# Products 6, 3 and 1 first for every expert, and one more wait for GpSimd's sums of w2

## The chip, the cores and the metric

The kernel runs on one core of one Trainium2 chip. The metric is the time of one execution on the device in microseconds (us), median of several runs. The core has TensorE (PE; its weight loads are PEld in the profile), VectorE (DVE), ScalarE (ACT), GpSimd (POOL), and SyncE (SP), which issues most DMAs.

## What is computed

Block-sparse attention (4 batches, 8 heads, 768 positions, 64 wide), and on its output x (3072 x 512) a mixture of 8 experts in which every token goes through every expert, weighted by a balanced gate P:

```python
logits = x @ w_gate
P = np.exp(logits - logits.max())
for _ in range(8):
    P /= P.sum(1, keepdims=True) + 1e-09
    P /= P.sum(0, keepdims=True) + 1e-09
    P *= N / E
for e in range(E):
    h = np.maximum(x @ w1[e], 0.0)
    out += P[:, e:e + 1] * (h @ w2[e])
```

w1 is 8 x 512 x 1024, w2 is 8 x 1024 x 512, all in fp32.

## The kernel before

**Attention** takes the first 412 us or so. Its order is written out by hand, and the change does not touch it: up to the last attention matmul all five engines have the same instructions in the same order before and after.

**The experts** follow as 32 tiles: tile i is expert e = i // 4 and batch b = i % 4 (768 tokens). Both layers use Strassen's scheme in Winograd's form: the operands are cut into 2 x 2 quadrants, and 7 products of sums of quadrants (named 0 to 6) take the place of 8. Every fp32 operand is split into a high and a low fp16 half, and a product takes three matmuls for each pair of blocks (high x high, high x low, low x high).

*First layer* (`stage1(i)`): each of the 7 products has 4 pieces q = 0 to 3 of 128 rows of h; one is a group of 6 matmuls of 384 columns into one of five PSUM banks `p_0` to `p_4` (line L1710; the pool "s1"). After a product a bank is read by ScalarE (`scaled_copy`, L1692, which starts a "pair" tile) or by VectorE (`scaled_add`, L1683, which adds the bank to a pair tile), and the next product adds to what stands in the same bank, so it waits for that reading. For experts 2 to 7 the products 6, 3, 1 and 2 are cut a second time into 7 inner products each (`inner_product`, STEPS, groups of 6 matmuls of 192 columns, L1739); they read further sums of w1 and x, kept in `loft`. `twos(e)` says which products that is: none for experts 0 and 1, (6, 3, 1, 2) for the others.

The other products run in an outer part: g = 0 takes q = 0, 1 and g = 1 takes q = 2, 3. Before, experts 0 and 1 take 0, 1, 5, 6, 4, 3, 2 there, for g = 0 and then for g = 1, without any overlap of the tiles' first layers. Experts 2 to 7 take 6, 3, 1, 2 as inner products first, and then 0, 5, 4; the half g = 1 is kept back and merged into product 6 of the next tile. `tokens()` writes this order down.

From the sums in the pair tiles (r, u, c; the bank itself holds a until all that needs it is done) ScalarE, VectorE and GpSimd make h with its own sums, as high halves (L1939, ScalarE) and low halves (L1930 on VectorE or L1928 on GpSimd, one or the other by the planner's choice). There are nine pair tiles and 24 h tiles.

*Second layer* (`stage2(i)`): 7 products in the order 1, 0, 5, 6, 3, 4, 2, each for 3 blocks of 128 tokens, a group of 12 matmuls of 256 columns (L2062) into one of three banks `y_0` to `y_2`. Results go to `acc` tiles and to DRAM.

**Weights.** `fetch_w1(e)` and `fetch_w2(e)` load a matrix into the one buffer `raw_w`, find its largest magnitude (8 pieces on ScalarE, L363; the maxima over the partitions go to DRAM and back as `peak_d` and `peaks`), make the sums of quadrants on GpSimd (`tts`, L1453) and split each product into `w1p[p]` or `w2p[p]` (high: ScalarE, L1465; low: VectorE, L1470). Product p of expert e can be split only when the last matmul of expert e - 1 on product p has run. For the inner products `inner(p, ...)` adds four sums on GpSimd and a second split (L1511, L1516). In `fetch_w2` the sums `d5` for product 5 write over m00, product 0's source, and wait for `zero`, product 0's split; `one` is product 1's split.

**x tiles.** `load_x(i + 1)` reloads the seven `xp[p]` from DRAM (L487), each after its last matmul in tile i. `prep_x` makes the inner sums of x once for the 16 pairs of batch and product (L1636 to L1673).

**The order on the engines** is set by a planner (`Plan.run`). It simulates the engines with fixed costs per job, takes on each engine the job with the earliest due time among those that are ready, and the instructions are then written in the order that comes out. On the chip each engine goes through its list in that order. SLK is the time after a group's planned end at which its bank shall have been read, SLK2 the same for the second layer, SHIFT the distance of the second layer behind the first, EASE an allowance for each group, MARGIN a factor on all costs but PE's and the DMAs', PREP0, PREP1 and PREPD the due times of `prep_x`.

Of the kernel before, what the change touches and what calls it, by code (L numbers as in the profile page):

```python
# [35 lines left out]
SLK, SLK2, SHIFT, EASE, SOON = 4, 2, 10, 0.2, 120.0  # L36
SLK3 = 20.0
PREP0, PREP1, PREPD = 100, 210, 50
# [3 lines left out]
LOADED = 5.0  # L42
WARM0, WARM1, WARM2 = 19, 5, 22
# [24 lines left out]
class Plan:  # L68
# [3 lines left out]
    MARGIN = 1.05  # L72
# [237 lines left out]
def tile_sparse_attention_moe(  # L310
# [1230 lines left out]
    def fetch_w2(e, loaded=None, done=None):  # L1541
# [26 lines left out]
        d5 = tts(m00, m11, t1, h2, tuple(zero), 0.73)  # L1568
# [127 lines left out]
    def stage1(i):  # L1696
# [140 lines left out]
        one, many, last = 1 in two, 6 in two, 2 in two  # L1837
        got = {}
        if many:
            got[6] = inner_product(6)  # L1840
            got[3] = inner_product(3, got[6])
        if one:
            got[1] = inner_product(1)
        if last:
            got[2] = inner_product(2)

        for g in range(NF // 2):
# [28 lines left out]
            first = lambda t, q: (t,)  # L1876
            prior = {}
            for q, (j, end) in outer(0, X, True, {}).items():
                if one:
                    r_[q] = scaled_add(cell(R, q), bank(X[q]), cell(R, q), [j] + rdep, dl=end + SLK)  # L1880
                    prior[q] = (r_[q],)
                else:
                    k = scaled_copy(cell(R, q), bank(X[q]), (j,), take=first(R, q), dl=end + SLK)
                    prior[q] = (k,)
            if not one:
                Z = {q: hold("s1") for q in qis}
                for q, (j, end) in outer(1, Z, True, {}).items():
                    r_[q] = scaled_add(
                        cell(R, q), bank(Z[q]), cell(R, q), (j,) + prior[q], drop=(Z[q],), dl=end + SLK
                    )  # L1890
            if not many:
                Y = {q: hold("s1") for q in qis}
            k5, k6 = {}, {}
            for q, (j, end) in outer(5, X, False, prior).items():
                if many:
                    c_[q] = scaled_add(cell(C, q), bank(X[q]), cell(C, q), [j] + cdep, dl=end + SLK)
                    k5[q] = c_[q]
                else:
                    k5[q] = scaled_copy(cell(C, q), bank(X[q]), (j,), take=first(C, q), dl=end + SLK)
# [369 lines left out]
```

## Time and profile before

| what | us |
|---|---|
| time, median of 3 runs (2136.47 to 2137.1) | 2136.53 |
| the profiled execution, its own time | 2137.5 |
| the span of that profile | 2135.7 |
| PE busy | 2113.9 |
| DVE busy | 1727.2 |
| ACT busy | 1431.2 |
| POOL busy | 1123.5 |

The span is what lies between the first and the last instruction; the 1.8 us between it and the execution's own time is not in the rows. Times in the rows are us from the span's start. A busy PE is a matmul in its pipeline: the end that a row shows for a group is about 0.16 us later than the moment at which the next group could begin, so an idle time of PE in a row is that much shorter than the gap between two groups.

### The profile page before, as it was taken

Reading aid. Unit: us, or ns where it says so; the run is one execution under the profiler, and the core shown is the slowest. Engines: PE = TensorE matmul, PEld = TensorE weight load, DVE = VectorE, ACT = ScalarE, POOL = GpSimd, SP = SyncE. Lnnn points to the kernel's source line nnn. Section 1 sums busy time; section 2 is a strip of 40 time slices with the busy share of each in tenths; the row PEclk is TensorE's granted clock in tenths of the full one; section 3 lists DMA queues with packets and bytes.
Section 4 is the critical chain, followed back from the end, with each engine's and each line's share of the span. In section 5 each row is a group of like instructions: output and inputs, shape, how many; then the busy total and the mean of one; then the engine's idle time right before and its main releaser. Section 6 shows DMA issues by size and latency. Waiting matters only on the chain.

```text
span 2135.7 us, 51438 instructions
## 1 busy us (share of the span) xinstructions
PE 2113.9 (99%) x20619; PEld 1711.2 (80%) x20619; DVE 1727.2 (81%) x3141; ACT 1431.2 (67%) x2785; POOL 1123.5 (53%) x1308
## 2 busy tenths in 40 slices
PE   9999999999999999999999999999999999999999
PEld 6777676667777778888888888888888888888888
DVE  8878889799778868877887888788878887888776
ACT  6788888886677656766676667656765676676442
POOL 6456768555345527644554456445644564456333
PEclk9999999999999999999999999999999999999999
DMA  7767866444446644464556455645554555455432
GB/s 160 146 137 160 213 137 141 149 125 139 150 154 188 183 135 146 152 148 112 136 129 153 112 139 126 151 112 146 124 146 112 151 129 136 112 166 150 142 97 68
DMA packets 225092, 299.79 MB, mean 140 GB/s; under 512 B 134332, under 2 KB 154708, under 8 KB 224852
## 3 DMA queue, kind: packets, MB, share of 16 engines
q1 hardware_dynamic: 218528, 265.02, 44.4%
q0 software_dynamic: 5760, 31.46, 9.1%
q8 instruction: 161, 2.64, 0.5%
q14 instruction: 79, 0.65, 0.1%
q10 hardware_dynamic: 564, 0.03, 0.0%
HBM read 198.15 MB, written 67.64 MB: 124 GB/s over the span
## 4 chain that ended last, share of the span: by engine, by line
PE 92%; DVE 4%; ACT 2%; DMA 1%; POOL 1%; issue 1%; SPq 0%; DVEq 0%; ACTq 0%
PE y L2062 41%; PE p L1710 23%; PE p L1739 15%; PE u L1056 4%; PE t L994 2%; PE t L989 2%; PE m L956 2%; PE m L959 2%; DVE top L965 1%; DMA qt<-qs 1%; ACT pe L999 0%; ACT unread L363 0%; PE u L1090 0%; POOL loft L548 0%; DVE pl L1009 0%
## 5 line engine op out<-in xcount | busy, mean ns | idle before, releaser
L2062 PE MATMUL y<-w2p,h 128*128 128x256 f16 x8064 | 980.7, 273 | 0.9 <-DVE h L1930 0.8
L2062 PEld LDWEIGHTS <-h 128*128 128x128 f16 x8064 | 784.5, 98 | 120.1 <-DVE h L1930 1.1
L1928 POOL TENSOR_TENSOR h<-pair,h 128x384 f16<-128x384 f32 x383 | 386.9, 1024 | 495.2 <-ACT h L1939 447.6
L1924 ACT ACTIVATE pair<-pair 128x384 f32<-128x384 f32 x384 | 198.2, 519 | 241.4 <-DVE pair L1683 239.9
L1710 PE MATMUL p<-arena 128*128 128x384 f16 x1728 | 322.3, 326 | 1.9 <-DVE pair L1683 1.9
L1939 ACT ACTIVATE h<-pair 128x384 f16<-128x384 f32 x640 | 303.7, 514 | 25.2 <-POOL pair L1970 13.2
L2101 DVE SCALAR_TENSOR_TENSOR acc<-y,spare,acc 128x256 f32<-128x256 f32 x408 | 201.6, 496 | 124.9 <-PE y L2062 116.6
L1683 DVE SCALAR_TENSOR_TENSOR pair<-p,pair 128x384 f32<-128x384 f32 x384 | 212.1, 553 | 81.3 <-PE p L1710 74.3
L1710 PEld LDWEIGHTS <-arena 128*128 128x128 f16 x1728 | 167.1, 98 | 84.6 <-issue 2.4
L999 ACT ACTIVATE pe<-t,qk 128x768 int32<-128x768 f32 x192 | 172.3, 899 | 64.5 <-PE t L994 57.2
L1710 PE MATMUL p<-attic 128*128 128x384 f16 x1152 | 213.6, 326 | 0.0
L1739 PEld LDWEIGHTS <-loft 128*128 128x128 f16 x2304 | 199.1, 98 | 16.2 <-issue 1.3
L965 DVE TENSOR_REDUCE top<-m 128x1 f32<-128x768 f32 x192 | 181.5, 951 | 37.4 <-PE m L959 36.4
L1930 DVE SCALAR_TENSOR_TENSOR h<-pair,h 128x384 f16<-128x384 f32 x257 | 187.0, 748 | 18.7 <-ACT h L1939 17.2
L1710 PEld LDWEIGHTS <-attic 128*128 128x128 f16 x1344 | 130.7, 98 | 66.4
L1739 PE MATMUL p<-loft 128*128 128x192 f16 x1728 | 181.3, 246 | 0.0
L1692 ACT ACTIVATE u<-p 128x384 f32<-128x384 f32 x216 | 105.5, 488 | 99.5 <-PE p L1739 75.8
L2089 ACT ACTIVATE acc<-y,spare 128x256 f32<-128x256 f32 (+1 forms) x180 | 97.7, 543 | 88.9 <-PE y L2062 79.4
L1453 POOL TENSOR_TENSOR raw_w<-raw_w 128x256 f32<-128x256 f32 (+1 forms) x150 | 130.4, 881 | 32.9 <-DVE attic L1470 14.7
L1013 POOL TENSOR_SCALAR pl<-pe 128x768 f16<-128x768 uint16 x109 | 93.3, 859 | 78.0 <-ACT pe L999 75.9
L989 PE MATMUL t<-qt,kt 128*128 128x512 f16 (+1 forms) x384 | 124.9, 325 | 3.6 <-DVE top L965 2.9
L1928 POOL TENSOR_TENSOR h<-u,h 128x384 f16<-128x384 f32 x91 | 89.9, 998 | 72.5 <-ACT h L1939 55.4
(249 smaller groups left out, 3856.4 us busy)
## 6 DMA issues: line engine op xcount, KB each, us to landing
arena<-xd SPq DMA_DIRECT2D x128, 384.0 KB, 3.8
attic<-xd SPq DMA_DIRECT2D x96, 384.0 KB, 3.3
loft<-xsd SPq DMA_DIRECT2D x96, 384.0 KB, 4.9
accd<-acc POOLq DMA_DIRECT2D x40, 768.0 KB, 9.1
raw_w<-in_moe_w_dram SPq DMA_DIRECT2D x28, 1024.0 KB, 5.7
accd<-acc SPq DMA_DIRECT2D x16, 768.0 KB, 4.1
acc<-accd SPq DMA_DIRECT2D x16, 768.0 KB, 4.4
xd<-loft SPq DMA_DIRECT2D x28, 384.0 KB, 2.9
```

What stands on the lines that cost most here:

```text
L965: nc.vector.tensor_reduce(out=tops[n][:, c : c + 1], in_=sc[:, :S], axis=AX.X, op=ALU.max)
L989: nc.tensor.matmul(sc[:, lo:hi], lhsT=kt[:, 0, c], rhs=qa[:, lo:hi], start=True, stop=False)
L999: nc.scalar.activation(pe, sc[:, :S], AF.Exp, bias=EXP_SHIFT, scale=qk[n // 2][3])
L1683: lambda: nc.vector.scalar_tensor_tensor(out=out_(), in0=bank_(), scalar=HDOWN, in1=add(), op0=ALU.mult, op1=ALU.add),
L1710: nc.tensor.matmul(bk.tile[:, :TH], lhsT=w1p[p][:, l, kc, fs], rhs=xp[p][:, r, kc], start=(fresh and kc == 0 and m == 0), stop=(kc == KH - ...
L1739: nc.tensor.matmul(bk.tile[:, c * HT : (c + 1) * HT], lhsT=lhs(l, c), rhs=rhs(rr), start=(fresh and c == 0 and m == 0), stop=(m == 2), ski ...
L1924: return job({"ACT": 0.52}, lambda: nc.scalar.activation(view(), view(), AF.Relu), dep)
L1928: nc.gpsimd.tensor_tensor(out=out_, in0=x, in1=y, op=ALU.subtract)
L1930: nc.vector.scalar_tensor_tensor(out=out_, in0=x, scalar=1.0, in1=y, op0=ALU.mult, op1=ALU.subtract)
L1939: lambda: nc.scalar.activation(h.tile[:, 0], src(), AF.Relu if relu else AF.Copy),
L2062: nc.tensor.matmul(py, lhsT=hh[i, p, kc].tile[:, l, tsl], rhs=w2p[p][:, r, kc], start=(old is None and kc == 0 and m == 0), stop=(kc == h2 ...
L2101: lambda dst=dst, src=src, t=t: nc.vector.scalar_tensor_tensor(out=dst(), in0=src(), scalar=pwe[e][:, t : t + 1] if e else 1.0, in1=dst(), ...
```

## The change

- For experts 0 and 1 the new function `front` runs product 6 and, in the same bank, product 3, first for q = 0, 1 and then for q = 2, 3; then it runs product 1 alone. ScalarE evacuates each of these pieces into pair tiles (6 pair tiles of a tile, as for experts 2 to 7). The outer part is now 0, 5, 4, 2 for these experts, with VectorE adding the bank to the pair tile after 0, 5 and 4 and ScalarE taking the bank after 2. A tile has as many matmuls, copies and adds as before.
- `tokens()` keeps back the half g = 1 for all experts and merges it into the products 6 and 3 of the next tile, from expert 1 to expert 2 too.
- `load_x` asks for 6, 3, 1, 2, 0, 5, 4 in this order.
- `d5` waits for `one` too.
- Constants: SLK 4 to 2.5, SLK2 2 to 5, SHIFT 10 to 11, EASE 0.2 to 0.3, PREP0 100 to 80, PREP1 210 to 170, MARGIN 1.05 to 1.08. DIRECT = 4 is new; it is compared with b, which is at most 3, so that `weighs` is `e` and `fresh` is as before.

```diff
-SLK, SLK2, SHIFT, EASE, SOON = 4, 2, 10, 0.2, 120.0
+SLK, SLK2, SHIFT, EASE, SOON = 2.5, 5, 11, 0.3, 120.0
...
-PREP0, PREP1, PREPD = 100, 210, 50
+PREP0, PREP1, PREPD = 80, 170, 50
...
+DIRECT = 4
...
-    MARGIN = 1.05
+    MARGIN = 1.08
...
-        d5 = tts(m00, m11, t1, h2, tuple(zero), 0.73)
+        d5 = tts(m00, m11, t1, h2, tuple(zero) + tuple(one), 0.73)
...
-        for p in PORDER:
+        for p in (6, 3, 1, 2, 0, 5, 4):
...
+        def front(chain):
+            sets = [[hold("pair") for _ in range(2)] for _ in chain]
+            made_ = [{}, {}]
+            for g in range(NF // 2):
+                qis = (2 * g, 2 * g + 1)
+                Y = {q: hold("s1") for q in qis}
+                prior = {q: () for q in qis}
+                for n, p in enumerate(chain):
+                    for q in qis:
+                        deps = list(prior[q])
...
+                        j, end = pe(
+                            (p, "q", q), start_group(p, q, Y[q], n == 0), NOUT, deps,
+                            take=(Y[q],) if n == 0 else (),
+                        )
...
+                        k = scaled_copy(
+                            lambda t=t, q=q: t.tile[:, q % 2], lambda q=q, Y=Y: Y[q].tile[:, :TH], (j,),
+                            take=(t,), drop=(Y[q],) if n == len(chain) - 1 else (), dl=end + SLK,
+                        )
+                        prior[q] = (k,)
...
+        if 6 in two:
             got[6] = inner_product(6)
             got[3] = inner_product(3, got[6])
-        if one:
+        else:
+            front((6, 3))
+        if 1 in two:
             got[1] = inner_product(1)
+        else:
+            front((1,))
...
-                steps = [p for p in (0, 1, 5, 6, 4, 3, 2) if p not in two]
+                steps = [p for p in (0, 5, 4, 2) if p not in two]
...
-            if 6 in two and 1 in two:
-                order += merge(inner[6], kept)
-                order += merge(inner[1], inner[3])
-                order += merge(inner.get(2, []), outer[0])
-                kept = outer[1]
+            if 6 in two:
+                order += merge(quarters[6], kept)
+                order += merge(lead[1], quarters[3])
             else:
-                order += kept
-                kept = []
-                for p in (6, 3, 1, 2):
-                    order += inner.get(p, [])
-                order += outer[0] + outer[1]
+                front = [t for g in (0, 2) for p in (6, 3) for t in halves(p, (g, g + 1))]
+                order += merge(front, kept)
+                order += lead[1]
+            order += merge(lead[2] if 2 in two else [], outer[0])
+            kept = outer[1]
         return order + kept
```

Lines after the change stand one later (L1692 is L1693) up to `front`, and six or seven later behind it (L1930 is L1936, L1970 is L1976, L2062 is L2069).

**Place A: ScalarE at the start of expert 0**, from the first split of the last x tile on (L1303 and L1304, into `loft`). L1692 and L1693 evacuate a bank `p`, L363 and L364 are pieces of w2's magnitude. Before:

```order
L1303 ACTIVATE loft_83<-loft_83 128x768 x2
L1692 ACTIVATE pair_0_8096<-p_0_8064 128x384
L1303 ACTIVATE loft_83<-loft_83 128x768
L1692 ACTIVATE pair_0_8096<-p_1_8065 128x384
L363 ACTIVATE unread_76,mx_w2_0_8172<-raw_w_4332 128x512 x3
L1692 ACTIVATE pair_1_8097<-p_0_8064 128x384
L363 ACTIVATE unread_76,mx_w2_0_8172<-raw_w_4332 128x512 x2
```

After:

```order
L1304 ACTIVATE loft_83<-loft_83 128x768
L1693 ACTIVATE pair_0_8096<-p_0_8064 128x384
L1304 ACTIVATE loft_83<-loft_83 128x768
L1693 ACTIVATE pair_0_8096<-p_1_8065 128x384
...
L1693 ACTIVATE pair_1_8097<-p_0_8064 128x384
L364 ACTIVATE unread_76,mx_w2_0_8171<-raw_w_4332 128x512
```

The bank `p_0`, product 0 before and product 6 after, is read after one split in place of two, and the evacuations stand between single pieces of the magnitude.

**Place B: PE in tile 0, from g = 0 to g = 1**, the first matmul of each group. Before, the rows are 2 (q = 0, 1; banks p_0 and p_1), 0 (q = 2, 3), 1 (q = 2; q = 3 follows in the same bank p_3) and 5 (q = 2):

```order
L1710 MATMUL p_0_8064<-attic_91 128x384
...
L1710 MATMUL p_1_8065<-attic_91 128x384
...
L1710 MATMUL p_4_8068<-arena_87 128x384
...
L1710 MATMUL p_2_8066<-arena_87 128x384
...
L1710 MATMUL p_3_8067<-arena_87 128x384
```

After, they are 2 (q = 0, 1; banks p_4 and p_0), then in turn product 6 of tile 1 (p_1), 0 of tile 0 for q = 2 (p_3), 6 of tile 1 (p_2), and 0 of tile 0 for q = 3:

```order
L1711 MATMUL p_4_8068<-attic_91 128x384
...
L1711 MATMUL p_0_8064<-attic_91 128x384
...
L1711 MATMUL p_1_8065<-arena_87,attic_91 128x384
...
L1711 MATMUL p_3_8067<-arena_87 128x384
...
L1711 MATMUL p_2_8066<-arena_87,attic_91 128x384
...
L1711 MATMUL p_4_8068<-arena_87 128x384
```

The last of these rows writes again the bank in which a of q = 0 stands (first row); before, the bank that was written twice in a row was p_3, with product 1.

**Place C: PE from expert 1 to expert 2**, the first matmul of each group. L1739 and L1740 are quarter products of tile 8. Before, from the last half product of tile 7 on:

```order
L1710 MATMUL p_4_8068<-attic_91 128x384
...
L2062 MATMUL y_2_8071<-w2p_4_8061,h_2_8074 128x256
...
L1739 MATMUL p_2_8066<-arena_87,attic_91 128x192
...
L1739 MATMUL p_3_8067<-arena_87,attic_91 128x192
...
L2062 MATMUL y_0_8069<-w2p_2_8059,h_3_8075 128x256
```

After, from the first quarter product of tile 8 on (L1711 are product 0 of tile 7 for q = 3 and product 5 for q = 2):

```order
L1740 MATMUL p_4_8068<-arena_87,attic_91 128x192
...
L1711 MATMUL p_3_8067<-arena_87 128x384
...
L2069 MATMUL y_1_8070<-w2p_5_8062,h_6_8078 128x256
...
L1740 MATMUL p_0_8064<-arena_87,attic_91 128x192
...
L2069 MATMUL y_2_8071<-w2p_5_8062,h_6_8078 128x256
...
L1711 MATMUL p_1_8065<-arena_87 128x384
```

Tile 8 begins while tile 7 still has seven of its half products ahead, at product 5 of the second layer of tile 6 in place of product 2, and its quarter products stand among those of tile 7.

## Rows read from the trace of the kernel before

**Rows 1.** The page's first two lines of busy time (span; each engine's busy time, share and instruction count) and the row of the clock that TensorE was granted in 40 slices of the span, in tenths.
```profile
span 2135.7 us, 51438 instructions
PE 2113.9 (99%) x20619; PEld 1711.2 (80%) x20619; DVE 1727.2 (81%) x3141; ACT 1431.2 (67%) x2785; POOL 1123.5 (53%) x1308
...
PEclk9999999999999999999999999999999999999999
```

**Rows 2.** The page's chain of work that ended last, its shares by engine.
```profile
PE 92%; DVE 4%; ACT 2%; DMA 1%; POOL 1%; issue 1%; SPq 0%; DVEq 0%; ACTq 0%
```

**Rows 3.** Busy time in stretches of 20 us: the stretch, its length, then busy us and instruction count of PE, PEld, DVE, ACT and POOL, the granted clock, the DMA share and GB/s. The start of expert 0, a stretch of expert 0 at speed, the change from expert 1 to expert 2, and the end.
```profile
420.00:440.00 20.00, 18.78 (x116) 11.20 (x115) 14.55 (x29) 19.60 (x51) 8.62 (x10) 1.00 0.41 84
...
460.00:480.00 20.00, 20.00 (x157) 15.13 (x156) 18.92 (x34) 13.42 (x28) 10.18 (x10) 1.00 0.51 166
...
820.00:840.00 20.00, 19.17 (x180) 16.67 (x178) 17.61 (x30) 15.32 (x27) 17.94 (x17) 1.00 0.58 197
...
940.00:960.00 20.00, 19.30 (x188) 16.98 (x186) 13.54 (x30) 8.78 (x20) 5.30 (x7) 1.00 0.84 193
...
2120.00:2140.00 20.00, 12.47 (x115) 10.93 (x112) 5.26 (x11) 0.00 (x0) 0.00 (x0) 0.93 0.18 60
```

**Rows 4.** Whom PE waited for, in us, number of waits and the longest, asked for four stretches one after the other: 398 to 470 us, 820 to 850, 850 to 900, 930 to 965. From 470 to 820 us PE waited for nobody.
```profile
PE p L1710 <- DVE pair L1683: 1.9, 2, 1.2
...
PE y L2062 <- DVE h L1930: 0.8, 1, 0.8
...
PE p L1739 <- DVE pair L1814: 0.3, 1, 0.3
...
PE p L1739 <- DVE pair L1814: 0.7, 1, 0.7
```

**Rows 5.** The chain of work that ended last, in order of time (start us, us, engine and line, matmuls): two whole groups of the second layer, two half products, four quarter products, each running without a gap.
```profile
582.98 2.62 PE y L2062 x24
589.83 1.95 PE p L1710 x12
...
1102.57 1.98 PE p L1739 x24
```

**Rows 6.** PE's timeline at the start of expert 0 (start us, us with the pipelined end of the last matmul, line, operation, tile, matmuls, and in brackets the idle time before).
```profile
411.87 1.14 PE L1710 MATMUL p<-arena 128*128 128x384 f16 x6
...
413.82 4.06 PE L1710 MATMUL p<-arena 128*128 128x384 f16 x24
...
427.10 3.09 PE L1710 MATMUL p<-arena 128*128 128x384 f16 x18
431.41 3.08 PE L1710 MATMUL p<-arena 128*128 128x384 f16 x18 [1.22 <-DVE pair L1683]
...
442.13 3.09 PE L1710 MATMUL p<-arena 128*128 128x384 f16 x18
445.94 0.32 PE L1710 MATMUL p<-arena 128*128 128x384 f16 x1 [0.72 <-DVE pair L1683]
```

**Rows 7.** ScalarE's timeline at the same place: the two copies of the last attention head, the first splits of the last x tile, an evacuation, and one of the eight pieces of w2's largest magnitude.
```profile
413.70 0.87 ACT L1100 ACTIVATE loft<-y 128x384 f32<-128x384 f32 x2 [3.02 <-PE y L1090]
414.45 1.58 ACT L1303 ACTIVATE loft<-loft 128x768 f16<-128x768 f32 x2
415.92 0.49 ACT L1692 ACTIVATE pair<-p 128x384 f32<-128x384 f32 x1
...
417.39 0.65 ACT L363 ACTIVATE unread<-raw_w 128x512 bf16<-128x512 f32 x1
```

**Rows 8.** VectorE's timeline there: the low halves of two splits, a sum in a bank, one low half of h alone, two of them beside GpSimd, and the reduction that waits for w2's peaks.
```profile
415.33 1.83 DVE L1306 TENSOR_TENSOR loft<-loft 128x768 f16<-128x768 f32 x2 [2.27 <-ACT loft L1303]
...
428.27 0.56 DVE L1970 TENSOR_TENSOR p<-p,pair 128x384 f32<-128x384 f32 x1
...
432.21 0.54 DVE L1930 SCALAR_TENSOR_TENSOR h<-u,h 128x384 f16<-128x384 f32 x1
...
433.61 1.82 DVE L1930 SCALAR_TENSOR_TENSOR h<-pair,h 128x384 f16<-128x384 f32 x2
...
439.88 0.28 DVE L459 TENSOR_REDUCE ma_w<-peaks 128x1 f32<-128x128 f32 x1
```

**Rows 9.** GpSimd's timeline beside the two low halves that stand last but one in rows 8.
```profile
432.66 0.92 POOL L1928 TENSOR_TENSOR h<-pair,h 128x384 f16<-128x384 f32 x1 [0.32 <-ACT h L1939]
433.83 1.19 POOL L1970 TENSOR_TENSOR pair<-pair,pair 128x384 f32<-128x384 f32 x1 [0.26 <-DVE pair L1970]
```

**Rows 10.** SyncE's queue: w2's peaks of expert 0 go out to DRAM and come back.
```profile
424.72 0.32 SPq L1435 DMA_DIRECT2D peak_d<-ma_w  x1
...
434.50 0.32 SPq L1439 DMA_DIRECT2D peaks<-peak_d  x1
```

**Rows 11.** w1 of expert 2, in order of time: the first split on ScalarE, the split of product 6 on ScalarE, and from the chain of waits the low half of the inner sums of product 1 on VectorE.
```profile
800.36 1.14 ACT L1465 ACTIVATE arena<-raw_w,sw 128x1024 f16<-128x1024 f32 x1
...
811.45 1.14 ACT L1465 ACTIVATE attic<-s,sw 128x1024 f16<-128x1024 f32 x1
...
845.69 2.04 DVE loft L1516
```

**Rows 12.** VectorE's longest stand at an x tile in 455 to 830 us (us, times, longest), and a low half of w2 of expert 0 on its timeline.
```profile
DVE loft L1636 <- DMA loft<-xd: 1.9, 1, 1.9
...
443.27 1.28 DVE L1470 SCALAR_TENSOR_TENSOR w2p<-raw_w,sw,w2p 128x1024 f16<-128x1024 f32 x1
```

More of the change, by code (lines that the diff above doesn't have):

```diff
@@ L1852, in stage1 @@
             M, mdep = made(2) if last else (None, [])
-            R, rdep = made(1) if one else (hold("pair"), [])
-            C, cdep = made(3) if many else (hold("pair"), [])
-            U, udep = made(6) if many else (hold("pair"), [])
+            R, rdep = made(1)
+            C, cdep = made(3)
+            U, udep = made(6)
             cell = lambda t, q: (lambda: t.tile[:, q % 2])
@@ L1874, in outer @@
                 return res
-            first = lambda t, q: (t,)
             prior = {}
             for q, (j, end) in outer(0, X, True, {}).items():
[L1879 to L1890, printed above, removed]
@@ L1891, in stage1 @@
-            if not many:
-                Y = {q: hold("s1") for q in qis}
-            k5, k6 = {}, {}
-            for q, (j, end) in outer(5, X, False, prior).items():
[L1895 to L1899, printed above, removed]
-            if not many:
-                for q, (j, end) in outer(6, Y, True, {}).items():
-                    k6[q] = scaled_copy(cell(U, q), bank(Y[q]), (j,), take=first(U, q), dl=end + SLK)
@@ L1903, in stage1 @@
-            for q, (j, end) in outer(4, X, False, {q: (k5[q],) for q in qis}).items():
-                u_[q] = scaled_add(
-                    cell(U, q), bank(X[q]), cell(U, q), [j] + (udep if many else [k6[q]]), dl=end + SLK
-                )
-                ends[q] = end
-            if not many:
-                for q, (j, end) in outer(3, Y, False, {q: (k6[q],) for q in qis}).items():
-                    c_[q] = scaled_add(
-                        cell(C, q), bank(Y[q]), cell(C, q), (j, k5[q]), drop=(Y[q],), dl=end + SLK
-                    )
+                r_[q] = scaled_add(cell(R, q), bank(X[q]), cell(R, q), [j] + rdep, dl=end + SLK)
@@ L1913, in stage1 @@
+                prior[q] = (r_[q],)
+            for q, (j, end) in outer(5, X, False, prior).items():
+                c_[q] = scaled_add(cell(C, q), bank(X[q]), cell(C, q), [j] + cdep, dl=end + SLK)
+            for q, (j, end) in outer(4, X, False, {q: (c_[q],) for q in qis}).items():
+                u_[q] = scaled_add(cell(U, q), bank(X[q]), cell(U, q), [j] + udep, dl=end + SLK)
+                ends[q] = end
             if last:
@@ L2025, in stage2 @@
         loaded = {}
-        fresh = e == 0 or ADDS <= e < NE - 1
+        fresh = e == 0 or ADDS <= e < NE - 1 or e == 1 and b >= DIRECT
+        weighs = e or b >= DIRECT
         if not fresh:
@@ L2089, in stage2 @@
                         lambda dst=dst, src=src, t=t: nc.scalar.activation(
-                            dst(), src(), AF.Copy, scale=pwe[e][:, t : t + 1] if e else 1.0
+                            dst(), src(), AF.Copy, scale=pwe[e][:, t : t + 1] if weighs else 1.0
                         ),
-                        rd + ([weighed[e]] if e else []), take=take, drop=drop, dl=at + SLK2,
+                        rd + ([weighed[e]] if weighs else []), take=take, drop=drop, dl=at + SLK2,
                     )
@@ L2101, in stage2 @@
                         lambda dst=dst, src=src, t=t: nc.vector.scalar_tensor_tensor(
[L2102 removed]
+                            out=dst(), in0=src(), scalar=pwe[e][:, t : t + 1] if weighs else 1.0,
                             in1=dst(), op0=ALU.mult, op1=ALU.add,
```

19 lines of the change are left out of this document (14 added, 5 removed).

## The prediction

> **What bounds the kernel now.** I read the page's busy times first: PE is busy for 2113.9 of 2135.7 us, no other engine for more than 81%, and TensorE's clock was granted in full in all 40 slices [rows 1], the higher of its two levels. The chain of work that ended last is PE for 92% [rows 2]. So the question is not which engine is fast, but where PE stands still, and the stretches of 20 us tell it [rows 3]: 20.00 of 20 us busy at 460 us, but 18.78 at 420, 19.17 at 820, 19.30 at 940, and the end. From 470 to 820 us PE waits for nobody [rows 4]. Where it runs, a group takes what its columns cost: 2.62 us for two groups of 12 x 256 columns (1.31 each), 1.95 for two of 6 x 384 (0.975), 1.98 for four of 6 x 192 (0.495) [rows 5]. The change leaves the number of groups of each kind as it is, so this part of the time, nearly all of it, can't move. What can move is the standing time around the experts, and of that there is little. At the start, PE waits twice for VectorE's reading of a bank, 1.22 and 0.72 us as shown [rows 6]. A shown idle time is 0.16 us too short: a group of 1.14 us in its row takes 0.975. The real gaps are thus 1.38 and 0.88, together **2.26**. From expert 1 to expert 2 PE waits 0.8, 0.3 and 0.7 [rows 4]; with 3 x 0.16 about **2.3**. The sum is 4.6 us, 0.2% of the time. That is the most that an order of the experts' work can give back, and 0.2% is also about what a measurement of this kernel can tell from no change. The end of the program (12.47 us busy in its last slice [rows 3]) has the same order before and after and stays.
>
> **The new front of experts 0 and 1.** The work per tile is the same: 28 groups of 0.975 and 21 of 1.31 us, 54.8 us, in experts 0 and 1. What is new is who has to be quick. Product 3 now adds to product 6's bank, so the third group of the first tile waits for ScalarE's copy of the first. Before, the second group of the same bank came seven groups of work later or had a bank of its own. I follow the start of tile 0 by hand, with the durations of the rows and the new order.
>
> (a) Product 6 for q = 0 starts at 411.87 as the first group does now, q = 1 starts at 413.82 and ends at 414.80 [rows 6]. ScalarE ends the last head's copies at 414.45, then makes one split of the x tile (1.58 for two, 0.79) and then the copy (0.49) [rows 7]: 414.45 + 0.79 + 0.45 = about 415.7. PE wants to begin product 3 at 414.80: a gap of 0.87. The copy of q = 1 stands behind a second split: 415.7 + 0.79 + 0.45 = 416.9 against 416.6 or so at which PE is through with q = 0 of product 3: I take 0.14. Later pieces of w2's magnitude (0.65 a piece [rows 7]) stand singly between the copies, and the groups alternate between banks, so that a copy has 0.975 + 0.975 us; no gap. Sum **1.0**.
>
> (b) From g = 0 to g = 1 (Place B) product 0 for q = 3 overwrites p_4, where a of q = 0 stands until VectorE has read it for the last time. On VectorE the sums there stand in this order behind the relu of both banks: the sum in p_4, then the reading of product 0 for q = 2, the sum in p_0, the low half from p_4, the low half of an x split, and only then the last reading of p_4. The second of these waits for PE's own group, product 0 for q = 2. From that group's end VectorE needs 0.56 + 0.56 + 0.54 + 0.92 + 0.56 = 3.1 us (a sum, a sum, a low half, half of the 1.83 for two splits' low halves, a sum) [rows 8], while PE has one group between (product 6 of tile 1, 0.975). Gap 3.1 - 0.98 = **2.2**.
>
> Together 3.2 in place of 2.26: **+0.9**. That tile 0's second layer begins some 8.5 us later costs nothing, since first-layer groups of tile 1 fill the place. The reduction that waits for w2's peaks stood at 439.88, 15.2 us after the peaks went out at 424.72 [rows 8, 10]. After, they go out about 3 us later, so the answer would be there at about 443, which is about when VectorE comes to it: no stall that PE sees. Bounds for the start as a whole: -1.3 (if the low half of x has run ahead and neither gap of (b) opens) to +2.5 (if the x split meets GpSimd's work).
>
> **VectorE beside GpSimd.** Two low halves of h took 1.82 us where one alone took 0.54, while GpSimd ran a low half of 0.92 and a sum of 1.19 beside them [rows 8, 9]; 0.74 us were lost. The Trainium skill, "SBUF — State Buffer", section "🔬 SBUF: two separate sides", has a rule for it: VectorE and GpSimd share a pair of ports that one instruction holds for itself, and the loser waits for all of it. That rule speaks against this change, and the row agrees with it: the loss is not a few per cent of a bandwidth. Four of the five steps in (b) read a bank and not two SBUF tiles; the x split does read two. Were it held up by one whole sum of GpSimd (1.19), the gap would be 3.4; this is a rival below.
>
> **From expert 1 to expert 2.** Before, tile 8's quarter products begin only when tile 7's first layer is through, the second layer's work between them is short, and PE comes too soon for the h tiles and for the sums in the bank [rows 4]. w1 of expert 2 is split from 800.36 on, product 6 is split at 811.45 and the inner sums of product 1 end at 845.69 + 2.04 [rows 11]. After, product 6 is last read by expert 1 near 763 us, 3 near 771 and 1 near 781 (groups counted from the start at their durations), and the first quarter product comes near 801, with seven half products of tile 7 and its second layer to mix in (Place C). Counted in the same way in the two orders (the durations of [rows 5]), tile 7's second layer then stands 12.5 and 19.9 us behind the last groups that its first two products need, the distances of the regular tiles where PE waits for nobody [rows 4]; before they were 9.7 and 13.6. So the three waits should go: **-2.3**. I leave **+0.3** for one short wait that stays. Bounds: -2.3 to +1 (a new wait for the inner sums, of the length of one of them, 2.04 [rows 11], half hidden).
>
> **Inside experts 0 and 1.** Here nothing can be gained, only lost. Each merged piece is followed on its bank after 2.3 to 3.7 us, some 6.9 before, counted likewise (at the nearest, in tile 0, 0.97). VectorE reads a bank in 0.56 [rows 8]; so 1.6 us of slack remain at the shortest. What can stand ahead on VectorE: a low half of w2, 1.28, and a stand at an x tile from DRAM, 1.9 us at the longest and once in 375 us [rows 12]. VectorE's share is already 18.92 of 20 us at 460 [rows 3]. The due times of the x sums come earlier (PREP0, PREP1), which packs them more tightly. One stand of 1.9 beyond a slack of 1.6 is 0.3; I allow **+0.5**, with 0 and +5 as ends.
>
> **Edits at nothing.** d5's wait for `one`: the low half of product 1 stands ahead of that of product 0 on VectorE, before and after, and an engine goes through its list in order; so `zero` is always the later of the two and the wait never ends last. Behind d5 on GpSimd are the sums for product 6 and the low halves of h; they lose nothing. The order of `load_x`: a product's x tile is free 20 to 34 us ahead of its next use in either order, so the later place of product 0 or 5 in SyncE's queue is covered; without that cover PE would stand by up to the 1.9 us of rows 12. DIRECT is never reached. SLK, SLK2, SHIFT, EASE and MARGIN act by the order alone, which I have read.
>
> **The sum.** 2136.53 + 0.9 - 2.3 + 0.3 + 0.5 = **2135.9 us**. The profiled execution took 2137.5, 1.0 above the median; the same sum from there gives 2136.9, and I count from the median.
>
> **The rivals.** *The waits from expert 1 to 2 stay*, because VectorE's inner sums and not the order held PE: 2136.53 + 0.9 + 0.5 = 2137.9. For it: both later waits are for VectorE's sums in pair tiles. Against: regular tiles with the same sums have none. *All stands go*: 2136.53 - 4.6 = 2131.9; against it are (a) and (b), which need ScalarE and VectorE to be quicker than their rows. *The slower side: VectorE's list runs into the shortened hand-overs.* Whenever a low half of w2 (1.28) and a stand at an x tile (1.9) come ahead of a piece's reading with 1.6 of slack, PE stands 1.6 us. Before, that was hidden by 6.9 us. There are 16 pairs of x tiles and products to prepare and two w2s in these 350 us; three such add 4.8 - 0.5 to the forecast, 2140.2, and from four on the time passes 0.2%. Half of the 16 would be 2148. Against: only one stand over 1 us was there, and reads of x come further ahead now. *GpSimd's lock on the way in (b)*: 2135.9 + 1.2 = 2137.1. *The change does not do what it says* holds for the wait of d5 alone, and is in the forecast.
>
> **How the numbers follow.** Forecast 0.57 (2134.5 to 2137), waits that stay 0.13, lock 0.06, all stands gone 0.1, VectorE's hand-overs 0.14. Faster by over 0.2% (below 2132.3) needs all stands gone, in full: 0.06. Slower by over 0.2% (above 2140.8) are most of the hand-over cases: 0.12. Within 0.2%: 0.82. The range from 2132.6 to 2140.0 leaves out most of the last two, under 2 in 10.
>
> **What would show it.** In the profile after: PE's idle times at the start are some 0.9 us behind a copy of ScalarE at 415 and some 2 us behind VectorE's reading of p_4 at 437, and none of 1.22 and 0.72 as before; from 820 to 965 PE waits for nobody, and the slices at 820 and 940 read 20.00. Waits of PE for VectorE's pair tiles or banks between 470 and 820 would show the hand-overs; waits at the same places as in rows 4, the first rival. The forecast is wrong if a slice elsewhere loses PE time, or if a group's duration in rows 5 changes.

## The result and the profile after

The changed kernel takes **2170.04 us** (median of 4 runs, 2159.59 to 2174.29) against 2136.5 before: 1.5% slower, ratio 1.015 with an interval of 1.0137 to 1.0164. The profiled execution took 2174.29, its span is 2172.5, 36.8 longer than that of before.

The page's first lines, as in [rows 1]:

```profile
span 2172.5 us, 51419 instructions
PE 2121.5 (98%) x20619; PEld 1715.3 (79%) x20619; DVE 1761.8 (81%) x3150; ACT 1432.5 (66%) x2785; POOL 1093.9 (50%) x1299
```

Three of the stretches of 20 us of [rows 3] (same columns), and three further on:

```profile
420.00:440.00 20.00, 17.82 (x110) 10.65 (x109) 10.65 (x21) 17.04 (x43) 9.35 (x11) 1.00 0.25 71
...
820.00:840.00 20.00, 20.00 (x200) 18.06 (x198) 18.91 (x32) 10.45 (x21) 11.17 (x12) 1.00 0.60 202
...
940.00:960.00 20.00, 20.00 (x194) 17.55 (x192) 13.16 (x31) 10.30 (x24) 4.05 (x5) 1.00 0.71 189
...
1100.00:1120.00 20.00, 13.26 (x111) 11.66 (x110) 17.10 (x15) 8.04 (x14) 11.01 (x15) 0.83 0.36 65
...
1540.00:1560.00 20.00, 13.26 (x110) 11.71 (x108) 16.84 (x15) 8.03 (x14) 10.91 (x14) 0.75 0.33 61
...
1760.00:1780.00 20.00, 13.26 (x128) 12.21 (x126) 18.32 (x18) 8.99 (x17) 14.77 (x19) 0.88 0.54 108
```

The kernel before was full in the last three; its first one, for instance:

```profile
1100.00:1120.00 20.00, 20.00 (x197) 17.79 (x195) 17.09 (x29) 14.11 (x27) 13.53 (x17) 1.00 0.69 164
```

Where the prediction looked, little was lost: the start reads 17.82 for 18.78, and the change from expert 1 to 2 (820 and 940) is now full. The loss is in stretches whose code nobody edited: at 1100, 1540 and 1760 us PE is busy for 13.26 of 20, and the mean granted clock there is 0.83, 0.75 and 0.88. Whom PE waited for (total, times, longest), in 398 to 470, 820 to 965, 1000 to 1400 and 1400 to 1800 us; in the last two it waited for nobody before:

```profile
PE p L1711 <- DVE pair L1976: 2.2, 1, 2.2
...
PE p L1711 <- ACT pair L1693: 0.8, 1, 0.8
...
PE p L1711 <- DVE pair L1793: 0.2, 1, 0.2
...
PE p L1740 <- DVE u L1777: 9.3, 4, 6.7
...
PE p L1740 <- DVE u L1777: 14.4, 4, 6.7
```

Line 1777 is a sum of VectorE in an inner product. What VectorE did ahead of it, in its timeline (L1471 is the low half of a split; the one at 1104.25 is that of w2's product 6, expert 3):

```profile
1100.81 1.27 DVE L1471 SCALAR_TENSOR_TENSOR w2p<-raw_w,sw,w2p 128x1024 f16<-128x1024 f32 x1
...
1104.25 9.92 DVE L1471 SCALAR_TENSOR_TENSOR w2p<-raw_w,sw,w2p 128x1024 f16<-128x1024 f32 x1
1114.10 0.54 DVE L1777 SCALAR_TENSOR_TENSOR u<-p,pair 128x384 f32<-128x384 f32 x1
```

An instruction that takes 1.27 us at 1100.81 (and 1.27 to 2.2 in every split of w2 in the kernel before) takes **9.92**. Below, an instruction that lasts so much longer than its own time is called held. Beside it GpSimd ran this, and then had nothing to do:

```profile
1102.89 0.89 POOL L2139 DMA_DIRECT2D accd<-acc  x1
1103.51 2.39 POOL L1454 TENSOR_TENSOR raw_w<-raw_w,t 128x256 f32<-128x256 f32 x3
1105.58 1.68 POOL L1454 TENSOR_TENSOR raw_w<-raw_w 128x256 f32<-128x256 f32 x2
1106.97 2.01 POOL L1934 TENSOR_TENSOR h<-pair,h 128x384 f16<-128x384 f32 x2
1108.85 1.00 POOL L1934 TENSOR_TENSOR h<-u,h 128x384 f16<-128x384 f32 x1
1109.72 1.48 POOL L1454 TENSOR_TENSOR raw_w<-raw_w 128x256 f32<-128x256 f32 x2
1111.08 2.00 POOL L1976 TENSOR_TENSOR pair<-pair,pair 128x384 f32<-128x384 f32 x2
```

GpSimd's last sum ends at 1111.08 + 2.00 = 1113.08, and VectorE's low half at 1104.25 + 9.92 = 1114.17, 1.09 later: about its own time. It was held until GpSimd was through. Note the first rows: the sums begin at 1103.51, while the DMA that GpSimd issues ahead of them runs to 1103.78, and each group in the list begins 0.1 to 0.3 us before the one ahead ends (1103.51 + 2.39 = 1105.90 against 1105.58).

The kernel before has holds too, short ones: beside two sums behind such a DMA a low half of w2 took 2.19 and ended 1.08 us after the second sum.

```profile
1105.14 2.19 DVE L1470 SCALAR_TENSOR_TENSOR w2p<-raw_w,sw,w2p 128x1024 f16<-128x1024 f32 x1
...
1105.05 1.20 POOL L1928 TENSOR_TENSOR h<-u,h 128x384 f16<-128x384 f32 x1
```

PE's timeline around the long hold, and the clock in stretches of 2 us:

```profile
1114.69 1.12 PE L1740 MATMUL p<-loft,attic 128*128 128x192 f16 x6 [6.74 <-DVE u L1777]
1115.61 1.17 PE L1740 MATMUL p<-loft 128*128 128x192 f16 x6
```

```profile
1110.00:1112.00 2.00, 0.00 (x0) 0.00 (x0) 2.00 (x1) 1.02 (x1) 2.00 (x3) 1.00 0.00 0
1112.00:1114.00 2.00, 0.00 (x0) 0.00 (x0) 2.00 (x1) 0.00 (x0) 1.08 (x2) 0.78 0.00 0
1114.00:1116.00 2.00, 1.31 (x9) 1.23 (x9) 1.66 (x4) 0.00 (x0) 0.00 (x0) 0.50 0.00 0
...
1118.00:1120.00 2.00, 2.00 (x13) 1.58 (x11) 0.48 (x1) 0.00 (x0) 0.00 (x0) 0.51 0.00 0
1120.00:1122.00 2.00, 2.00 (x23) 1.86 (x21) 1.75 (x2) 0.49 (x1) 0.00 (x0) 1.00 0.18 28
```

PE stands for 6.74 us. In the slices the granted clock is 1.00 while it stands, falls to 0.78 and then to 0.50, the lower level (1.2 GHz), and is back at 1.00 after 1120. While it was low, six matmuls of 192 columns took 0.92 us (from 1114.69 to 1115.61) in place of 0.495. So PE pays twice for each of the three long holds. The fourth one, of 4.94 us in expert 4 (at 1327.80), cost it a wait of 1.76 and left the clock at 1.00.

The sum of the rows: behind 820 us PE's waits come to 28.8 us against 1.8 before (9.3 and 14.4 of it in the rows above), the start to 3.0 against 1.9, and PE's busy time grew by 7.6: 27.0 + 1.1 + 7.6 = 35.7 of the 36.8. Most of the 7.6 is the lower clock: behind the three long waits 15.2 us of matmuls ran at 0.50, half of which is lost (the kernel before lost 1.7 in this way, 8 us from its start, which the digits of [rows 1] can't show: a 9 is 90% or more). The pipelined ends of the groups ahead of 17 more waits, 0.16 us each, are in it as well.

### The profile page after: what moved, and what is told of

The parts are those of the page before. It is cut to its first block, busy times and chain, and to the rows that moved or that the text cites. A ratio compares the mean times of both kernels' runs of the same rounds, so it can differ in the third digit from the quotient of the medians.

```text
span 2172.5 us, 51419 instructions
## 1 busy us (share of the span) xinstructions
PE 2121.5 (98%) x20619; PEld 1715.3 (79%) x20619; DVE 1761.8 (81%) x3150; ACT 1432.5 (66%) x2785; POOL 1093.9 (50%) x1299
## 4 chain that ended last, share of the span: by engine, by line
PE 90%; DVE 5%; issue 2%; ACT 1%; DMA 1%; POOL 1%; SPq 0%; ACTq 0%; DVEq 0%
PE y L2069 40%; PE p L1711 23%; PE p L1740 14%; PE u L1057 4%; PE t L995 2%; PE t L990 2%; PE m L957 2%; PE m L960 2%; DVE top L966 1%; DMA qt<-qs 1%; DVE h L1936 1%; DVE arena L1471 0%; ACT pe L1000 0%; DVE u L1777 0%; PE u L1091 0%
## 5 line engine op out<-in xcount | busy, mean ns | idle before, releaser
L2069 PE MATMUL y<-w2p,h 128*128 128x256 f16 x8064 | 975.8, 273 | 0.0
L2069 PEld LDWEIGHTS <-h 128*128 128x128 f16 x8064 | 786.6, 98 | 117.0
L1934 POOL TENSOR_TENSOR h<-pair,h 128x384 f16<-128x384 f32 x354 | 352.9, 1017 | 490.0 <-ACT h L1945 327.8
L1945 ACT ACTIVATE h<-pair 128x384 f16<-128x384 f32 x640 | 310.6, 516 | 39.4 <-PE y L2069 21.4
L1711 PE MATMUL p<-arena 128*128 128x384 f16 x1728 | 324.6, 326 | 2.4 <-DVE pair L1976 2.2
L1930 ACT ACTIVATE pair<-pair 128x384 f32<-128x384 f32 x384 | 199.4, 520 | 186.9 <-DVE pair L1684 184.9
L1711 PEld LDWEIGHTS <-arena 128*128 128x128 f16 x1728 | 167.6, 98 | 85.4 <-issue 2.8
L1936 DVE SCALAR_TENSOR_TENSOR h<-pair,h 128x384 f16<-128x384 f32 x286 | 199.6, 711 | 32.1 <-ACT h L1945 31.3
L1740 PEld LDWEIGHTS <-loft 128*128 128x128 f16 x2304 | 201.3, 99 | 21.0 <-issue 9.0
L1711 PE MATMUL p<-attic 128*128 128x384 f16 x1152 | 215.8, 326 | 0.8 <-ACT pair L1693 0.8
L1740 PE MATMUL p<-loft 128*128 128x192 f16 x1728 | 181.1, 248 | 5.9 <-ACT u L1693 3.6
L1693 ACT ACTIVATE u<-p 128x384 f32<-128x384 f32 x216 | 105.4, 488 | 122.8 <-PE p L1740 111.4
L1711 PEld LDWEIGHTS <-attic 128*128 128x128 f16 x1344 | 130.2, 98 | 68.3 <-issue 1.2
L1454 POOL TENSOR_TENSOR raw_w<-raw_w 128x256 f32<-128x256 f32 (+1 forms) x150 | 123.2, 836 | 43.4 <-ACT unread L364 27.9
L1740 PEld LDWEIGHTS <-attic 128*128 128x128 f16 x1296 | 113.3, 98 | 34.3 <-issue 22.6
L1693 ACT ACTIVATE pair<-p 128x384 f32<-128x384 f32 x168 | 80.7, 486 | 88.3 <-PE p L1740 49.8
```

The source lines that it names most:

```text
L1693: lambda: nc.scalar.activation(out_(), bank_(), AF.Relu if relu else AF.Copy, scale=HDOWN),
L1711: nc.tensor.matmul(bk.tile[:, :TH], lhsT=w1p[p][:, l, kc, fs], rhs=xp[p][:, r, kc], start=(fresh and kc == 0 and m == 0), stop=(kc == KH - ...
L1740: nc.tensor.matmul(bk.tile[:, c * HT : (c + 1) * HT], lhsT=lhs(l, c), rhs=rhs(rr), start=(fresh and c == 0 and m == 0), stop=(m == 2), ski ...
L1930: return job({"ACT": 0.52}, lambda: nc.scalar.activation(view(), view(), AF.Relu), dep)
L1934: nc.gpsimd.tensor_tensor(out=out_, in0=x, in1=y, op=ALU.subtract)
L1936: nc.vector.scalar_tensor_tensor(out=out_, in0=x, scalar=1.0, in1=y, op0=ALU.mult, op1=ALU.subtract)
```

## The experiments

Theory A, at first: VectorE's instructions with two operands in SBUF are held while GpSimd runs back to back, and the constants put the low half of product 6 there. Its rivals were the front and the merging (B), a wait of the low half's own (C) and the mere place in VectorE's list (D).

**Which part of the change.** e1 takes the constants back, e2 puts them alone into the kernel before:

```diff
-SLK, SLK2, SHIFT, EASE, SOON = 2.5, 5, 11, 0.3, 120.0
+SLK, SLK2, SHIFT, EASE, SOON = 4, 2, 10, 0.2, 120.0
-PREP0, PREP1, PREPD = 80, 170, 50
+PREP0, PREP1, PREPD = 100, 210, 50
-    MARGIN = 1.08
+    MARGIN = 1.05
```

> The changed kernel with the six planner constants of before (SLK, SLK2, SHIFT, EASE, PREP0 and PREP1, MARGIN); the new front, the merging and the wait in d5 stay. Theory A (VectorE's low half of w2's product 6 is held while GpSimd runs its sums and low halves of h back to back, and it is the constants that put it there): the low half of product 6 now stands behind that of product 5 in VectorE's list, none lasts over 3 us, time 2133 to 2139. Rival B (the new front and the merging themselves leave VectorE too late, whatever the constants): long low halves and waits of PE stay, 2155 to 2175.

> The kernel before with the six new planner constants alone. Theory A: the low half of product 6 moves ahead of that of product 5, into GpSimd's run of sums, lasts 5 to 10 us in several experts, PE waits for VectorE there, time 2150 to 2175. Rival B (front and merging): no such hold, 2134 to 2139.

e1: 2134.33 against 2135.67 (0.9994, interval 0.9985 to 1.0004), no low half of w2 over 2.11 us. e2: 2156.14 (1.0096, 1.0079 to 1.0113). The constants cost the time, in either kernel, and the front costs none; B falls. In detail e2 was a miss: its low half of product 6 was held for only 2.75, because GpSimd's run ended soon, and the time went in 17 waits of PE for VectorE behind 820 us, 17.2 us in all and none over 1.5.

e7 takes one constant back (`MARGIN = 1.05`).

> The changed kernel with MARGIN alone back at 1.05. From VectorE's list: product 6's low half now stands behind the four sums that PE waits for and not ahead of them, while GpSimd's sums still stand in a row. Theory A: low halves may still be held for 3 to 8 us, but with little behind them that PE needs at once; 2136 to 2152. If the other constants do it on their own: 2155 to 2175.

2139.27 (1.0015, 1.0006 to 1.0024); no low half of w2 over 2.53 us, although 3 to 8 had been allowed for, and five waits of up to 0.8. MARGIN alone, taken back, gives back most of the loss; the other constants were not taken apart.

**What holds VectorE.** e3 and e4 gave the planner one more dependency:

```diff
 e3
-        d5 = tts(m00, m11, t1, h2, tuple(zero) + tuple(one), 0.73)
+        d5 = tts(m00, m11, t1, h2, tuple(zero) + tuple(one) + tuple(six), 0.73)
 e4
-        six = put(6, m01, d6)
+        six = put(6, m01, tuple(d6) + tuple(d5))
```

> The changed kernel, with GpSimd's sums d5 waiting for the split of product 6 as well, so that GpSimd stands until VectorE's low half is done and its run begins after it. Theory A: the low half of product 6 lasts 1.3 to 2.5 us, the waits of 6.7 us are gone, time 2136 to 2145 (some waits of 0.7 us may stay). Rival C (the long record is the low half's own wait, for ScalarE's high half or for a buffer, and GpSimd beside it is chance): it stays long and so does PE's wait, 2155 to 2175.

> The changed kernel, with the split of w2's product 6 waiting for d5 on top of its own sums, so that both its halves come later. Theory A: most of GpSimd's run is over when the low half comes, it lasts 1.3 to 3 us, time 2136 to 2147. Rival C: its own wait is still there, 2155 to 2175.

e3: 2189.95 (1.0256), slower still and a miss for theory A; e4: 2147.15 (1.0056, 1.0041 to 1.0071), no low half of w2 over 2.09, and the time just above theory A's range. e3 looked like a point for C, but its trace says otherwise. VectorE's low half of product 6 and GpSimd's last sum of that run:

```profile
1109.45 10.51 DVE L1471 SCALAR_TENSOR_TENSOR w2p<-raw_w,sw,w2p 128x1024 f16<-128x1024 f32 x1
...
1117.66 1.20 POOL L1976 TENSOR_TENSOR pair<-pair,pair 128x384 f32<-128x384 f32 x1
```

The low half ends at 1119.96, GpSimd's run at 1118.86: again 1.10 later, now after 10.51 us, since the run was longer. And d5 had run beside the low half it was to wait for: such a dependency orders the planner's list, but the chip did not wait for it. e5 adds data, one column of the low half that GpSimd copies ahead of d5:

```diff
+            nc.gpsimd.tensor_copy(out=c, in_=w2p[6][:, 1, 0, 0:1])
```

> The kernel of e3_d5_waits_for_product_6 with one more instruction: ahead of d5 GpSimd copies one column of the low half of w2's product 6 into a scratch tile, so that it really waits for VectorE (in e3 the wait stood in the planner alone, and on the chip d5 ran beside the low half). Nothing else is left out. Theory A (VectorE is held as long as GpSimd runs without a pause): no low half of product 6 is held longer than two of GpSimd's instructions ahead of the wait take (under 4 us), PE's waits of over 5 us are gone, time 2138 to 2152 against 2190 for e3. Rival C (the low half waits for something of its own): as e3, 2180 to 2195.

2146.07 (1.0044, 1.0027 to 1.0061), longest low half of w2 2.44. C falls: with GpSimd standing, the low half has nothing of its own to wait for. e4 and e5 still lie 10 to 11 us above the kernel before. Five holds of 3.1 us at low halves of w1, which the changed kernel has as well, are left in both, and PE's waits behind 820 us come to 7.6 in e4.

e6 moves the low half of product 6 ahead of that of 5 in e1 and leaves GpSimd's list mixed:

```diff
-        five = put(5, m00, d5)
+        five = put(5, m00, tuple(d5) + tuple(six))
```

> The kernel of e1 (old constants) with one rule for the planner added: product 5's split comes after product 6's, so that VectorE's list has the low half of 6 ahead of that of 5 as in the changed kernel. GpSimd's sums stay mixed with low halves of h for which it waits for ScalarE. Theory A (it takes a run of GpSimd without a pause, the place alone does nothing): no low half over 3 us, 2133 to 2140. Rival D (the place ahead of product 5 is enough): holds of 5 to 10 us, 2150 to 2175.

2136.31 (0.9998, 0.9989 to 1.0008), longest 2.01: the place alone does nothing, D falls.

**The hold by itself.** e8 runs the two instructions alone.

> A kernel that computes nothing of the reference (its output is zeros): in rounds, GpSimd gets 0, 1, 2, 4, 8 or 12 sums of 128 x 256 back to back, and VectorE, 0.5 us after their start, one instruction: the low half of w2 (two operands in SBUF, 1.27 us alone), a low half of h (two in SBUF, 0.55), a sum with a bank (one in SBUF, 0.56) or a scaling with one operand. In a last round GpSimd has two sums and VectorE eight low halves of h. Theory A: the instructions with two operands in SBUF last until GpSimd's run ends and their own time more (with 8 sums of 0.73 about 6.5 us, with 12 about 9.5); those with a bank last 0.56 as ever. If the lock is handed over after each instruction of GpSimd: at most 0.8 us more than alone, whatever the run. Rival C: no change at all with the run.

Here theory A failed. VectorE's low half beside 12 sums, and GpSimd's 12 sums:

```profile
48.26 1.37 DVE L90 SCALAR_TENSOR_TENSOR B<-A,z,B 128x1024 f16<-128x1024 f32 x1
...
47.82 9.18 POOL L121 TENSOR_TENSOR G<-C,E 128x256 f32<-128x256 f32 x12 [0.54 <-DVE C L118]
```

1.37 us in place of the 9.5 expected; GpSimd gave way instead (9.18 for 12 sums that take 0.68 each, so it lost 1.0). A run without a pause doesn't hold VectorE. What e8 lacked stands in the rows of after: a DMA that GpSimd issues itself, and behind it sums that start before the one ahead has ended. Behind 470 us, holds of more than 1.6 us over the shortest time of the same line and shape number nine in after, thirteen in e3 and fifteen in e2, and none in before, e1 and e7. All of them lie in such a run. The short ones follow the same pattern. In these six kernels 104 of VectorE's instructions with two operands in SBUF begin inside such a run, nine of them in before. Of these, 103 end 0.42 to 0.43 or 1.09 us after the run's last sum, which is about their own time; the exception is the hold of 4.94 in after. The change made no new kind of wait: it put a low half beside a run of twelve sums. That is theory A2, and e9 asks for it:

```diff
+        nc.gpsimd.dma_start(out=Z[r], in_=W, accum_op=ALU.add)
         for k in range(count):
             nc.gpsimd.tensor_tensor(out=G[:, g], in0=C[:, 0:256], in1=E[:, 0:256], op=ALU.subtract)
```

> As e8, a kernel that computes nothing of the reference. Rounds of 2, 4, 8 or 12 back-to-back sums of GpSimd, now directly behind a DMA that GpSimd itself issues (0.89 us; it adds a tile to DRAM as the kernel's stores of acc do); one such round with a drain of GpSimd between the DMA and 8 sums; two rounds of 8 sums without a DMA. Theory A2 (in e8 VectorE got its turn after one sum; the traces of after, e2 and e3 show every hold of over 1.6 us in a run of GpSimd that follows such a DMA without a pause, each sum starting 0.3 us before the end of the one ahead): behind a DMA the low half of w2 lasts to the end of the run, about 1.5 us with 2 sums, 3 with 4, 5.5 with 8, 8 with 12; without a DMA, and with the drain, 1.3 to 2.0. A low half of h is held likewise, a sum with a bank is not. Rival: the DMA changes nothing, 1.3 to 2.0 in all rounds.

VectorE's instruction in the first nine of eleven rounds: 8 sums without a DMA; 2, 4, 8 and 12 sums behind one; 8 behind a DMA and a drain; then behind a DMA with 8 sums a low half of h, a sum with a bank, a scaling with one operand in SBUF. Below, GpSimd's list in the round of 8 behind a DMA:

```profile
29.03 1.53 DVE L98 SCALAR_TENSOR_TENSOR B<-A,z,B 128x1024 f16<-128x1024 f32 x1
...
37.30 1.91 DVE L98 SCALAR_TENSOR_TENSOR B<-A,z,B 128x1024 f16<-128x1024 f32 x1
...
41.88 3.14 DVE L98 SCALAR_TENSOR_TENSOR B<-A,z,B 128x1024 f16<-128x1024 f32 x1
...
47.69 5.84 DVE L98 SCALAR_TENSOR_TENSOR B<-A,z,B 128x1024 f16<-128x1024 f32 x1
...
56.20 8.62 DVE L98 SCALAR_TENSOR_TENSOR B<-A,z,B 128x1024 f16<-128x1024 f32 x1
...
67.50 1.27 DVE L98 SCALAR_TENSOR_TENSOR B<-A,z,B 128x1024 f16<-128x1024 f32 x1
...
80.97 5.18 DVE L102 SCALAR_TENSOR_TENSOR B<-A,B 128x384 f16<-128x384 f32 x1
...
88.93 0.56 DVE L106 SCALAR_TENSOR_TENSOR D<-pb,D 128x384 f32<-128x384 f32 x1
...
96.28 5.32 DVE L110 TENSOR_SCALAR B<-A 128x1024 f16<-128x1024 f32 x1
```

```profile
46.02 0.88 POOL L141 DMA_DIRECT2D Z<-W  x1
46.63 5.74 POOL L129 TENSOR_TENSOR G<-C,E 128x256 f32<-128x256 f32 x8
52.06 1.71 POOL L135 COPY G<-E 128x256 f32<-128x256 f32 x1
```

1.53 without; 1.91, 3.14, 5.84, 8.62 behind the DMA, 0.62 to 0.70 for each further sum, about a sum's own pace. The last two rounds repeat 8 sums without and with the DMA: 1.45 and 6.15. The round with the drain decides nothing: its low half had ended at 68.77, and the sums came only at 72.72:

```profile
72.72 5.48 POOL L129 TENSOR_TENSOR G<-C,E 128x256 f32<-128x256 f32 x8 [5.94 <-issue]
```

The low half of h (0.54 alone) takes 5.18 and the scaling (0.68 in e8) 5.32; the sum with a bank 0.56, as ever. Again the sums start at 46.63 while the DMA runs to 46.90. The hold ends with the sums, not with the run: the copy behind them starts at 52.06, ahead of their end at 52.37, like a sum, but it gave way and lasts 1.71 (0.39 in the rounds without a DMA), and the low half ends at 53.53.

**In the kernel.** e10 and e11 put a drain of GpSimd behind each DMA, e12 three tiny copies that wait for each other:

```diff
 e10, e11
+        nc.gpsimd.drain()
 e12
+        nc.gpsimd.tensor_copy(out=c[0], in_=inv_v[:, 0:1])
+        nc.gpsimd.tensor_copy(out=c[1], in_=c[0])
+        nc.gpsimd.tensor_copy(out=c[2], in_=c[1])
```

> The changed kernel with one edit: a drain of GpSimd behind each of its 40 DMAs, so that the next instruction starts only when the DMA is through. Order, constants and front are those of the changed kernel. Theory A2: no low half over 3 us, the waits of 6.7 us gone, the clock full throughout, time 2134 to 2142. Rival (long runs of GpSimd hold VectorE with or without a DMA ahead): 2155 to 2175.

> e1 (the new front with the old constants) with the same drains. In e1 five holds of 1.7 us are left, behind DMAs, and no wait of PE hangs on them: both theories expect 2132 to 2137. It is run as the version that could beat both kernels.

> The changed kernel with three copies of 128 x 1 on GpSimd behind each of its 40 DMAs, each copy waiting for the one ahead (GpSimd does nothing for a moment, but doesn't wait for the DMA's own end as the drain did, 7 us). The planner knows nothing of them: every engine's order is that of the changed kernel. Theory A2: the next sums no longer start ahead of the end of the one before, no low half lasts over 3 us, PE's waits of 6.7 us are gone and with them the half clock behind them; 2135 to 2145. Rival (the drain of e10 removed the holds only because GpSimd came so late; the order alone makes the hold): 2155 to 2175.

e10: 2258.54 (1.0579), e11: 2325.16 (1.0879), both misses. The longest low half of w2 in e10 is 1.95, so the holds are gone, but a drain behind a DMA keeps GpSimd idle for some 6 us (5.86 and 6.14 at two of them in e10, 5.94 in e9), and PE waits 38.6 us for GpSimd's low halves of h. e12: **2134.68** against 2135.29 (0.9994, 0.9985 to 1.0003). Its PE waits from 398 us on, the same low half of product 6, and GpSimd's list beside it:

```profile
PE p L1711 <- DVE pair L1976: 2.2, 1, 2.2
PE p L1711 <- ACT pair L1693: 0.8, 1, 0.8
```

```profile
1102.48 1.28 DVE L1471 SCALAR_TENSOR_TENSOR w2p<-raw_w,sw,w2p 128x1024 f16<-128x1024 f32 x1
...
1101.12 0.89 POOL L2027 DMA_DIRECT2D accd<-acc  x1
...
1102.52 1.28 POOL L2032 COPY gap<-gap 128x1 f32<-128x1 f32 x1
1103.76 2.09 POOL L1454 TENSOR_TENSOR raw_w<-raw_w,t 128x256 f32<-128x256 f32 x3
1105.82 1.41 POOL L1454 TENSOR_TENSOR raw_w<-raw_w 128x256 f32<-128x256 f32 x2
...
1109.82 2.40 POOL L1454 TENSOR_TENSOR raw_w<-raw_w 128x256 f32<-128x256 f32 x2
...
1109.49 1.45 DVE L1471 SCALAR_TENSOR_TENSOR w2p<-raw_w,sw,w2p 128x1024 f16<-128x1024 f32 x1
```

With every engine's order and all constants as in the changed kernel, 120 tiny copies give back 35 us. The sums now start 0.03 us ahead of the end of the group before (1103.76 + 2.09 = 1105.85 against 1105.82), the low half takes 1.28, and PE waits from 398 us on for the two gaps of the new front and 0.5 us more. This low half ran ahead of the sums: GpSimd's third copy, of one column, gave way and took 1.28. But a later one, at 1109.49, lies inside the same run of sums and takes 1.45; there two sums gave way and took 2.40 in place of 1.41. No instruction of VectorE is held for more than 1.6 us in e12, those at w1 included. e1 and e12 are level with the kernel before; no version beats both kernels clearly.

## Why the prediction was wrong

- **The sum's own terms held.** Start: 0.77 and 2.18 as shown, with 0.16 each 3.3, for 3.2 forecast (1.0 and 2.2). The second gap of (a) did not come; its own figures, 416.9 against 416.6, would have made it 0.3 and not 0.14. Expert 1 to 2: one wait of 0.2 is left, for 0.3 forecast. Inside experts 0 and 1: nothing. The reduction for w2's peaks came at 443.01, for "about 443". e12, the changed kernel without the holds, is 0.6 us below the kernel before, and the sum said 0.6; e12's interval goes from 3.2 us below to 0.6 above, so this agreement is partly luck.
- **The step that failed** is "SLK, SLK2, SHIFT, EASE and MARGIN act by the order alone, which I have read", and with it the first section's "this part of the time, nearly all of it, can't move". The constants stand in the sum at nothing, and they cost some 35 us (2170.04 with them, 2134.33 without, e1). The order was read where the code was edited, at the start and from expert 1 to 2. In experts 3 to 6 the constants moved the low half of product 6 to a place ahead of the sums that PE waits for, beside a run of twelve sums behind a DMA on GpSimd. No rival covered that: the largest time named was 2148. The prediction's own sign of being wrong, a slice elsewhere that loses PE time, is what came.
- **The price of the lock** was the second error. The prediction took one whole sum of GpSimd (1.19) as the most that VectorE can lose, and put it at one place. The price was the rest of the run: 8.65 us over VectorE's 1.27. The Trainium skill's "SBUF — State Buffer", section "🔬 SBUF: two separate sides", speaks of a pair of ports held for one whole instruction. e8 fits it (1.37 beside 12 sums, so it waited for less than one sum of 0.68); e9, after, and e3 differ as soon as a DMA of GpSimd stands ahead, and there the measurement decides.
- **The rival on the slower side** named VectorE's list as the bound, and rightly, but in experts 0 and 1, as many small stands; it was three large ones and a smaller one in experts 3 to 6, with the lower clock behind the three.
- d5's wait for `one` was rightly put at nothing: without it the lists of all engines are row for row the same, so there was nothing to run.

Shown: that a DMA which GpSimd issues directly ahead of a run of sums makes the hold (e9, with and without it), and that three tiny copies between the two, with every engine's order kept, give the time back (e12). Argued: that the early start of each sum is how VectorE is never let in. Against its being enough stand the hold of 4.94 in expert 4 and the copy in e9: both let VectorE in although they had started 0.13 and 0.31 us before the end of the row ahead. Not settled: why they did; whether it is the wait of each copy for the one ahead or the copies themselves that help in e12; whether another DMA than one that adds to DRAM holds likewise; what the constants other than MARGIN do.

The four times of the changed kernel lie near 2174, 2174, 2167 and 2160, some 7 us apart. A full hold costs PE 5.0 us more of standing than the one of 4.94 (6.74 against 1.76), and by the clock 2.0 to 3.0 us, estimated from the matmuls that ran at 0.50. One more hold that ends early in each step would account for the spread, but this is not shown: the rows are of the slowest of the four.

## What to carry to other kernels

When a planner's constants change, every stage changes, and the steady ones, which fill most of the time, have to be compared first. Where VectorE and GpSimd both work on SBUF, look on GpSimd's list for its own DMA issues and for what stands directly behind them; in this kernel three tiny copies there, each waiting for the one ahead, cost nothing that the time shows and VectorE got its turn (e12), while drains ended the holds but cost 88 us on top of the changed kernel (e10). Such a hold is priced by the rest of the run, not by one instruction.

## What the runs showed of the hardware

- Behind a DMA that GpSimd issues, VectorE's instruction with two operands in SBUF lasted to the end of GpSimd's sums (1.91, 3.14, 5.84, 8.62 us for 2, 4, 8, 12 sums in e9; 103 of 104 cases in six kernels); without the DMA 1.37 beside 12 sums (e8). With one operand in a bank it was not held (0.56); a scaling of one fp32 operand in SBUF into fp16 was (5.32).
- A drain of GpSimd behind its DMA left it idle for some 6 us (5.94 in e9; 5.84 at the least behind the 40 DMAs of e10).
- While PE stood for 6.74 us, from about 1108 to 1114.69, the granted clock fell from 1.00 to 0.50 (1.00 in the slice from 1110 on, 0.78 in the one from 1112 on), and it was back at 1.00 at 1120, some 5 us after PE had begun again.
